# Value products of a cycle in two halves of 256 queries, with the output half in the first half's bank

## The chip, the cores and the metric

The kernel runs on one core of a Trainium2 chip. The metric is the device time of one execution in microseconds. The kernel before takes 947.69 us (median of three runs, 947.59 to 947.73). Its profile was taken in one execution of 946.93 us, of which the trace covers a span of 945.1 us; the mean granted TensorE clock was 0.997.

Engines are named as in the profile: PE is TensorE's matmul, PEld its weight load, DVE VectorE, ACT ScalarE, POOL GpSimd, SP SyncE.

## What is computed

The reference gates two branches over 2048 tokens of width 448. Branch A is attention with 16 query heads of 28 and a single key and value head, followed by an output projection; branch B is a token-shift mixer with two MLPs.

```python
q = (x @ wq).reshape(B, S, H, Dh)          # H = 16, Dh = 28
k = x @ wk; v = x @ wv                     # one head for all queries
p = softmax(einsum("bhqd,bkd->bhqk", q, k) * Dh ** -0.5)
a = einsum("bhqk,bkd->bhqd", p, v).reshape(B, S, H * Dh) @ wo
g = sigmoid((x * gate_w).sum(-1, keepdims=True))
return g * a + (1 - g) * b                 # b: the mixer, B_ref(x, ...)
```

## The kernel before

All arithmetic is in 32-bit floats; the score products run as three products of split operands (high by high, low by high, high by low). A first stage projects queries and the mixer's first half, a second one, up to about 400 us, runs the mixer's MLP. The change lies in the third stage, the attention, from there to the end.

**Units and cycles.** A unit u (0 to 15) is a block of 512 queries (u // 4) and a group of four heads (u % 4). Keys come in 16 tiles of 128. A cycle c handles two key tiles of a unit, so a unit has 8 cycles (i = 0 to 7) and the stage 128. The order of the work is written by hand; each engine runs its instructions in that order, and a tile framework adds the waits between engines.

**Banks.** PSUM has four single banks (`singles`) and two pairs of banks (`pairs`). Cycle c calls the singles s0, s1, s2, s3; in the next cycle the two halves of the list change places, so its s2 and s3 are this cycle's s0 and s1.

**One cycle, in PE's order.**

- A, the scores of the even key tile: heads 0 and 1 into s0 and s1, heads 2 and 3 into `pairs[0]`. Twelve matmuls (line 203), in three rounds of four; the four of a round use four row groups of the array.
- B, the same for the odd key tile, into s2, s3 and `pairs[1]`.
- V, the value products of the cycle before (line 861): for its two key tiles and four heads, `vext` (128 keys by 32 columns, one of which is ones and gives the softmax sum) against the probabilities of 512 queries, into the four column groups of s0. A 32-bit matmul of this kind is two instructions in the trace, so these are 16.
- W, a "job" (line 813): half of an output product, 224 of 448 columns of `wo` for 128 tokens, into s1. It is eight instructions. A unit's eight jobs are added to the list at i=4 of the next unit and are taken one in a cycle, two at i=5 (`TWICE`), none at i=2; the first unit has eight jobs of the mixer's last product (line 840) in their place, and the last one takes two a cycle from i=4.
- At i=2 (`MAX_AT`) there is in place of a job a product for the next unit's maxima (line 210), into s1.

**The other engines in a cycle.** ACT runs six exponentials (line 850): s0, s1, s2, s3, `pairs[1]`, each out of PSUM, and the two heads of `pairs[0]`, which DVE has copied to SBUF (line 889). DVE runs that copy, then the add of V's bank to the sum `o` of the unit (line 787, or a copy at the first time, line 785), then the job's add (line 832, or 844 for the mixer's). Between the copy and the add it has at i=1 a check and a reciprocal of the sums (lines 778 and 799), at i=3 the arrangement of the maxima (lines 236 to 240) and the normalisation (line 808), and at i=6 the split of the queries of a later unit (lines 194 and 195). At i=0 the SP queue sends the finished sums of the unit before out of `o` (`sums_begin`, line 792); after the add of the right half of an output tile's last group it sends the tile to the output (line 835).

Of the kernel before, what the change touches and what calls it, by code (L numbers as in the profile page):

```python
# [18 lines left out]
D = 448  # L19
# [5 lines left out]
NT = S // P  # L25
NF = F // P
NE = D // 32
NG = H // 4
# [13 lines left out]
def gated_mix_kernel(  # L42
# [12 lines left out]
    nc = tc.nc  # L55
# [688 lines left out]
    with tc.tile_pool(name="s3", bufs=1, reuse_waits="tile") as s3, \  # L744
# [8 lines left out]
        def bank(name):  # L753
            ps = banks.pop(0)
            banks.append(ps)
            return ps
# [20 lines left out]
            g = good[:, c:c + sums.shape[1]]  # L777
            nc.vector.scalar_tensor_tensor(g, sums, LIMIT, g, op0=ALU.is_le, op1=ALU.min)

        o_of = {}  # L780

        def values_end(u, pv):
            if u not in o_of:
                o_of[u] = s3.tile([P, 512], F32, tag="o", bufs=2, name=f"o_{u}")
                nc.vector.tensor_copy(o_of[u], pv)
            else:
                nc.vector.tensor_add(o_of[u], o_of[u], pv)  # L787

        def sums_begin(u):
            o = o_of.pop(u)  # L790
            rt = s3.tile([P, 16], F32, tag="rt", bufs=2, name=f"rt_{u}")
            nc.sync.dma_start(rt, o[0:128:32, :].rearrange("j (a b) -> j a b", b=16))
            return u, o, rt
# [16 lines left out]
        def by_columns(ps, a, t, w):  # L810
            for i in range(4):
                c = t * P + 32 * i
                nc.tensor.matmul(ps[32 * i:32 * i + 32, :], a[:, c:c + 32], w, start=True, stop=True,  # L813
                                 tile_position=(0, 32 * i))
# [3 lines left out]
        halves = [slice(0, D // 2), slice(D // 2, D)]  # L818

        def wo_products(u, t, ps, cols=whole):  # L820
            by_columns(ps[:, cols], on_of[u], t, wof[:, u % NG, cols])

        def wo_add(u, t, ps, cols=whole, end=None):
            b, g = divmod(u, NG)
            n = 4 * b + t
            before = x1[:, n, :] if g == 0 else ot_of[n]
            if g == 0 and cols.start == 0:
                ot_of[n] = s3.tile([P, D], F32, tag="ot", bufs=6, name=f"ot_{n}")
            if end:
                end(t, n, ps[:, cols], before)  # L830
                return
            nc.vector.scalar_tensor_tensor(ot_of[n][:, cols], ps[:, cols], gg[:, n:n + 1], before[:, cols],
                                           op0=ALU.mult, op1=ALU.add)
            if g == NG - 1 and cols.stop == D:
                nc.sync.dma_start(out[0, n * P:(n + 1) * P, :], ot_of[n])
# [1 line left out]
        weigh_x1(NT - 4, NT)  # L837

        def w4_products(t, ps, cols):
            by_columns(ps[:, cols], gf_late, t, w4_late[:, cols])  # L840

        def w4_add(t, ps, cols):
            n = NT - 4 + t
            nc.vector.scalar_tensor_tensor(x1[:, n, cols], ps[:, cols], gi[:, n:n + 1], x1[:, n, cols],
                                           op0=ALU.mult, op1=ALU.add)

        p_of = {}
# [6 lines left out]
            p_of[u * NT + kt] = p = s3.tile([P, 4, 512], F32, tag="p", bufs=PB, name=f"p_{u}_{kt}")  # L854
            return p

        def values(k, pv, first, last):
            u, kt = divmod(k, NT)
            p = p_of.pop(k)
            for j in range(4):  # L860
                nc.tensor.matmul(pv[32 * j:32 * j + 32, :], vext[:, kt, :], p[:, j],  # L861
                                 start=first, stop=last, tile_position=(0, 32 * j))

        jobs = [(w4_products, w4_add, (t,), cols) for t in range(4) for cols in halves]
        left, right, both = slice(0, 1), slice(1, 2), slice(2, 4)
# [2 lines left out]
        MAX_AT = 2  # L868
        TWICE = 5

        def run_jobs(ps, n):
            adds = []
            for _ in range(min(n, len(jobs))):
                products, add, args, cols = jobs.pop(0)
                products(*args, ps, cols)
                adds.append((add, args, cols))
            for add, args, cols in adds:
                add(*args, ps, cols)

        NC = NU * NT // 2  # L880
        for c in range(NC):
            u, i = divmod(c, NT // 2)
            k = 2 * c
            s0, s1, s2, s3_ = singles if c % 2 == 0 else singles[2:] + singles[:2]
            pa = score_tiles(u, 2 * i, s0, s1, pairs[0])
            exps(pa, left, s0.unsqueeze(1))
            exps(pa, right, s1.unsqueeze(1))
            if c < NC - 1:
                nc.vector.tensor_copy(pa[:, both], pairs[0])  # L889
            else:  # L890
                exps(pa, both, pairs[0])
            while later:
                later.pop(0)()
            if i == 1 and sums:
                norms.append(recip(*sums.pop()))
            if i == 1 and u == 0:
                q_begin(1)
                q_fetch(2)
            if i == 3 and norms:
                w = norms[0][0]  # L900
                norm(*norms.pop())
            if i == 6 and u + 2 < NU:
                q_begin(u + 2)
                q_fetch(u + 3)
            pb = score_tiles(u, 2 * i + 1, s2, s3_, pairs[1])
            exps(pb, left, s2.unsqueeze(1))
            exps(pb, right, s3_.unsqueeze(1))
            exps(pb, both, pairs[1])
            if c < NC - 1:
                exps(pa, both)  # L910
            if c:
                v = (c - 1) // (NT // 2)
                values(k - 2, s0, True, False)
                values(k - 1, s0, False, True)
                values_end(v, s0)
                if i == 0 and v < NU - 1:
                    sums.append(sums_begin(v))
            if i == 4 and u:
                jobs += [(wo_products, wo_add, (u - 1, t), cols) for t in range(4) for cols in halves]
            if i == MAX_AT and u + 1 < NU:  # L920
                max_part(u + 1, range(4), s1)
                later.append(lambda u=u: max_end(u + 1))
            elif c == 0:
                run_jobs(s0, 2)
                run_jobs(s1, 2)
            else:
                run_jobs(s1, 2 if i == TWICE or (u == NU - 1 and i > 3) else 1)
        pv = pairs[0][:, 0]
        values(2 * NC - 2, pv, True, False)
        values(2 * NC - 1, pv, False, True)  # L930
        assert not sums and not norms and not jobs and not later

        u = NU - 1
# [30 lines left out]
        def end(t, n, ps, before):  # L964
            if t == 1:
                nc.scalar.activation(y, ps, AF.Copy, scale=gg[:, n:n + 1])
                nc.gpsimd.tensor_tensor(ot_of[n], y, before, ALU.add)
            else:
                nc.vector.scalar_tensor_tensor(ot_of[n], ps, gg[:, n:n + 1], before, op0=ALU.mult, op1=ALU.add)
            queue = nc.scalar if t == 1 else nc.sync  # L970
            queue.dma_start(out[0, n * P:(n + 1) * P, :], ot_of[n])

        def tail_wo(t):
            wo_products(u, t, wo_banks[t])
            wo_add(u, t, wo_banks[t], end=end)

        def keep_warm(n):
            for _ in range(n):
# [39 lines left out]
        with tc.If(again > 0, label="redo"):  # L1018
            for b in range(NB):
                for g in range(NG):  # L1020
                    u = b * NG + g
                    q_fetch(u)
                    q_begin(u)
                    max_full(u, bank)
                    max_end(u)
                    pv = banks.pop(0)
                    for kt in range(NT):
                        ps = [bank(f"s2_{u}_{kt}_{j}") for j in range(4)]
                        scores(u, kt, ps)
                        p = s3.tile([P, 4, 512], F32, tag="p", bufs=PB, name=f"p2_{u}_{kt}")  # L1030
                        for j in range(4):
                            exps(p, slice(j, j + 1), ps[j].unsqueeze(1))
                        p_of[u * NT + kt] = p
                        values(u * NT + kt, pv, kt == 0, kt == NT - 1)
                    values_end(u, pv)
                    banks.append(pv)
                    norm(*recip(*sums_begin(u), False))
                    for t in range(4):
                        ps = bank(f"wo2_{u}_{t}")
                        wo_products(u, t, ps)  # L1040
                        wo_add(u, t, ps)

# [50 lines left out]
```

## Time and profile before

| | us |
|---|---|
| median of the runs (3) | 947.69 |
| profiled execution | 946.93 |
| its span | 945.1 |
| PE busy (modelled) | 936.3 |
| DVE busy | 504.1 |
| ACT busy | 637.3 |

A unit's eight cycles, u13 from 829.53 to 862.73 us, as busy time of the engines in each cycle (the columns are the stretch, its length, then busy time and instructions that began in it for PE, PEld, DVE, ACT and POOL, the granted clock, the share of the DMA engines and GB/s):

```
829.53:833.58 4.05, 4.05 (x52) 1.85 (x49) 2.28 (x4) 3.91 (x7) 0.00 (x0) 1.00 0.02 4
833.58:837.63 4.05, 4.05 (x52) 1.85 (x48) 2.60 (x6) 3.93 (x7) 0.00 (x0) 1.00 0.19 61
837.63:841.90 4.27, 4.27 (x48) 2.11 (x44) 2.50 (x4) 4.14 (x7) 0.00 (x0) 1.00 0.18 63
841.90:845.98 4.08, 4.08 (x49) 1.84 (x48) 3.33 (x8) 3.72 (x7) 0.00 (x0) 1.00 0.01 2
845.98:850.05 4.07, 4.07 (x52) 1.85 (x49) 2.29 (x4) 3.92 (x7) 0.00 (x0) 1.00 0.03 6
850.05:854.48 4.43, 4.43 (x62) 2.12 (x58) 2.66 (x4) 4.29 (x7) 0.00 (x0) 1.00 0.15 56
854.48:858.67 4.19, 4.19 (x53) 1.84 (x49) 3.35 (x7) 3.68 (x7) 0.00 (x0) 1.00 0.00 0
858.67:862.73 4.06, 4.06 (x53) 1.86 (x49) 2.29 (x4) 3.79 (x7) 0.00 (x0) 1.00 0.01 4
```

In an answer in order of time, a row has the start, the duration, the engine, the line, the operation with its tiles and form and, in brackets, how long the engine had stood idle before it and what ended that. Rows of one kind that lie close together are merged, with a count. A wait row has who waited for whom, the total in us, the number of times and the longest.

### The profile page before, as it was taken

What the parts mean: (1) busy time and instruction counts of PE and PEld (TensorE: products, weight loads), DVE (VectorE), ACT (ScalarE), POOL (GpSimd) and SP (SyncE); (2) the same over time, 40 slices, a digit from 0 to 9 for tenths busy, and PEclk for the clock granted to TensorE, in tenths of its full rate; (3) what the DMA queues carried; (4) which work ended last, traced back from release to release, by engine and by line L of the source; (5) the groups of instructions that cost most, each with busy time, mean ns of one, the idle gap of its engine ahead of it and who ended that gap; (6) DMA issues with size and microseconds to landing.
All of it is one profiled execution on the core that took longest, in us unless ns stands there. A gap on an engine that the chain in (4) does not pass through costs nothing.

```text
span 945.1 us, 19526 instructions
## 1 busy us (share of the span) xinstructions
PE 936.3 (99%) x8085; PEld 585.7 (62%) x8085; DVE 504.1 (53%) x829; ACT 637.3 (67%) x1006; POOL 80.8 (9%) x111
## 2 busy tenths in 40 slices
PE   9999999999999999999999999999999999999997
PEld 6788888888888888843444444444444444444442
DVE  4664464432432421266666666666656666666654
ACT  5532444322222222299999999999999999999993
POOL 3342500200000420110000000000000000000000
PEclk9999999999999999999999999999999999999998
DMA  9833452300300300010000000000010000010001
GB/s 313 283 83 76 138 167 85 93 10 1 84 1 1 84 1 1 12 50 24 12 23 14 23 32 33 24 13 23 15 51 23 14 23 12 31 40 16 6 13 43
DMA packets 40423, 47.05 MB, mean 50 GB/s; under 512 B 10120, under 2 KB 28488, under 8 KB 40328
## 3 DMA queue, kind: packets, MB, share of 16 engines
q1 hardware_dynamic: 37304, 40.27, 13.9%
q10 hardware_dynamic: 3024, 5.47, 1.6%
q8 instruction: 65, 1.06, 0.5%
q14 instruction: 30, 0.25, 0.1%
HBM read 32.56 MB, written 11.67 MB: 47 GB/s over the span
## 4 chain that ended last, share of the span: by engine, by line
PE 97%; ACT 1%; DMA 0%; DVE 0%; issue 0%; DVEq 0%
PE bank L861 24%; PE bank L203 22%; PE bank L813 5%; PE acc L682 5%; PE acc L684 5%; PE acc L683 5%; PE g L135 4%; PE g L136 4%; PE g L137 4%; PE pair L203 3%; PE hs L460 1%; PE hs L461 1%; PE g L138 1%; PE g L139 1%; ACT p L850 1%; PE h L135 1%
## 5 line engine op out<-in xcount | busy, mean ns | idle before, releaser
L850 ACT ACTIVATE p<-bank 128x512 f32<-128x512 f32 x512 | 265.1, 607 | 32.5 <-PE pair L203 17.3
L861 PE MATMUL bank<-p,vext 128*32 128x512 f32 x2032 | 244.3, 598 | 0.1
L889 DVE COPY p<-pair 128x1024 f32<-128x1024 f32 x127 | 155.5, 1225 | 22.7 <-PE pair L203 19.8
L672 ACT ACTIVATE gh<-g 128x512 fp32r<-128x512 f32 x55 | 32.9, 598 | 184.7 <-PE g L139 184.7
L787 DVE TENSOR_TENSOR o<-o,bank 128x512 f32<-128x512 f32 x111 | 76.3, 687 | 149.0 <-PE bank L861 135.1
L203 PE MATMUL bank<-qh,kh 32*128 32x512 f32 x512 | 146.3, 471 | 0.0
L850 ACT ACTIVATE p<-p 128x1024 f32<-128x1024 f32 x127 | 139.2, 1096 | 0.0
L850 ACT ACTIVATE p<-pair 128x1024 f32<-128x1024 f32 x129 | 136.8, 1060 | 0.0
L203 PE MATMUL bank<-ql,kh 32*128 32x512 f32 x512 | 130.6, 396 | 0.0
L861 PEld LDWEIGHTS bank<-p,vext 128*32 128x32 f32 x2032 | 53.0, 109 | 122.5 <-issue 76.0
L203 PE MATMUL pair<-qh,kh 32*128 32x512 f32 x512 | 128.0, 496 | 0.3 <-DVE x L738 0.3
L674 DVE TENSOR_TENSOR gl<-gf,gh 128x512 fp32r<-128x512 f32 x55 | 38.2, 695 | 166.5 <-ACT gf L673 166.5
L203 PE MATMUL bank<-qh,kl 32*128 32x512 f32 x512 | 126.9, 388 | 0.0
L203 PEld LDWEIGHTS bank<-qh,kh 32*128 32x128 f32 x512 | 69.0, 182 | 75.3 <-ACT p L850 40.9
L203 PE MATMUL pair<-qh,kl 32*128 32x512 f32 x512 | 101.0, 389 | 0.0
L203 PE MATMUL pair<-ql,kh 32*128 32x512 f32 x512 | 100.5, 387 | 0.0
L682 PE MATMUL acc<-w4h,gh 128*128 128x448 f32 x220 | 80.3, 365 | 0.0
L684 PE MATMUL acc<-w4h,gl 128*128 128x448 f32 x220 | 80.0, 364 | 0.0
L683 PE MATMUL acc<-w4l,gh 128*128 128x448 f32 x220 | 80.0, 363 | 0.0
L203 PEld LDWEIGHTS bank<-qh,kl 32*128 32x128 f32 x512 | 69.6, 183 | 8.4
L813 PEld LDWEIGHTS bank<-wof,on 128*32 128x32 f32 x992 | 32.0, 110 | 64.4 <-issue 32.1
L813 PE MATMUL bank<-wof,on 128*32 128x224 f32 (+1 forms) x992 | 67.5, 359 | 0.0
(199 smaller groups left out, 1470.3 us busy)
## 6 DMA issues: line engine op xcount, KB each, us to landing
qd<-qf ACTq DMA_DIRECT2D x16, 256.0 KB
rb<-rd SPq DMA_DIRECT2D x15, 256.0 KB
x<-in_x_dram SPq DMA_DIRECT2D x4, 896.0 KB
xd<-xt SPq DMA_DIRECT2D x16, 224.0 KB
w34raw<-in_w_dram SPq DMA_DIRECT2D x7, 512.0 KB
qr<-qd SPq DMA_DIRECT2D x64, 56.0 KB
out_dram<-ot SPq DMA_DIRECT2D x15, 224.0 KB
w34raw<-in_w_dram SPq DMA_DIRECT2D x7, 448.0 KB
```

Source lines behind the costliest of these rows:

```text
L135: nc.tensor.matmul(ps, wh[:, c, :], ah[:, c, :], start=(c == 0), stop=False)
L136: nc.tensor.matmul(ps, wh[:, c, :], al[:, c, :], start=False, stop=False)
L203: nc.tensor.matmul(ps[j], k[h, keys], q[h, :], start=(r == 0), stop=(r == 2), tile_position=(32 * j, 0))
L674: nc.vector.tensor_sub(gl, gf, f32(gh))
L682: nc.tensor.matmul(ps, gh[:, tok], w4h[i][:, k, :], start=(f == 0), stop=False)
L683: nc.tensor.matmul(ps, gh[:, tok], w4l[i][:, k, :], start=False, stop=False)
L684: nc.tensor.matmul(ps, gl[:, tok], w4h[i][:, k, :], start=False, stop=(f == stop))
L787: nc.vector.tensor_add(o_of[u], o_of[u], pv)
L813: nc.tensor.matmul(ps[32 * i:32 * i + 32, :], a[:, c:c + 32], w, start=True, stop=True, tile_position=(0, 32 * i))
L850: nc.scalar.activation(p[:, heads], p[:, heads] if source is None else source, AF.Exp, scale=SCALE)
L861: nc.tensor.matmul(pv[32 * j:32 * j + 32, :], vext[:, kt, :], p[:, j], start=first, stop=last, tile_position=(0, 32 * j))
L889: nc.vector.tensor_copy(pa[:, both], pairs[0])
```

## The change

In the cycles that have at most one job and no maxima, the value products run in two halves. Queries 0 to 255 of both key tiles go to the first 256 columns of s0, and DVE adds them to the first half of `o`. Queries 256 to 511 go to the first 256 columns of s1. The job's products come next, into columns 256 to 479 of s0, which the values no longer use; then DVE adds s1 to the second half of `o`, and then the job's result. Before, all values went to s0 and the job to s1, and DVE added them in that order. In these cycles V is 32 instructions of 256 columns in place of 16 of 512, and DVE has two adds of 256 columns in place of one of 512.

Cycles with two jobs (i=5, and from i=4 in the last unit) and those with the maxima (i=2) keep the one product of 512 queries. Where a unit begins (i=0), the DMA of the finished sums is now issued after the job's work, and not before it. The functions of the jobs take the part of the bank they write, in place of the bank and the columns; the path that repeats the attention with exact maxima, which runs only if a sum was out of range, is adapted to that.

```diff
-        o_of = {}
-        def values_end(u, pv):
+        o_of, fresh = {}, set()
+        def values_end(u, pv, qs=slice(0, 512)):
             if u not in o_of:
                 o_of[u] = s3.tile([P, 512], F32, tag="o", bufs=2, name=f"o_{u}")
-                nc.vector.tensor_copy(o_of[u], pv)
+                fresh.add(u)
+            o = o_of[u][:, qs]
+            if u in fresh:
+                nc.vector.tensor_copy(o, pv)
+                if qs.stop == 512:
+                    fresh.remove(u)
             else:
-                nc.vector.tensor_add(o_of[u], o_of[u], pv)
+                nc.vector.tensor_add(o, o, pv)
...
-        def values(k, pv, first, last):
-            u, kt = divmod(k, NT)
-            p = p_of.pop(k)
-            for j in range(4):
-                nc.tensor.matmul(pv[32 * j:32 * j + 32, :], vext[:, kt, :], p[:, j],
-                                 start=first, stop=last, tile_position=(0, 32 * j))
+        def values(ks, pv, qs=slice(0, 512)):
+            for k in ks:
+                u, kt = divmod(k, NT)
+                for j in range(4):
+                    nc.tensor.matmul(pv[32 * j:32 * j + 32, :], vext[:, kt, :], p_of[k][:, j, qs],
+                                     start=(k == ks[0]), stop=(k == ks[-1]), tile_position=(0, 32 * j))
+                if qs.stop == 512:
+                    p_of.pop(k)
...
-        def run_jobs(ps, n):
+        def job_products(ps, n):
             adds = []
             for _ in range(min(n, len(jobs))):
                 products, add, args, cols = jobs.pop(0)
-                products(*args, ps, cols)
-                adds.append((add, args, cols))
-            for add, args, cols in adds:
-                add(*args, ps, cols)
+                part = ps[:, 0:D // 2] if n == 1 else ps[:, cols]
+                products(*args, part, cols)
+                adds.append((add, args, part, cols))
+            return adds
...
-            if c:
-                v = (c - 1) // (NT // 2)
-                values(k - 2, s0, True, False)
-                values(k - 1, s0, False, True)
-                values_end(v, s0)
-                if i == 0 and v < NU - 1:
-                    sums.append(sums_begin(v))
...
-            if i == MAX_AT and u + 1 < NU:
-                max_part(u + 1, range(4), s1)
-                later.append(lambda u=u: max_end(u + 1))
-            elif c == 0:
+            if c == 0:
                 run_jobs(s0, 2)
                 run_jobs(s1, 2)
+                continue
+            v = (c - 1) // (NT // 2)
+            most = 2 if i == TWICE or (u == NU - 1 and i > 3) else 1
+            at_max = i == MAX_AT and u + 1 < NU
+            if at_max or (most == 2 and jobs):
+                values((k - 2, k - 1), s0)
+                values_end(v, s0)
+                if at_max:
+                    max_part(u + 1, range(4), s1)
+                    later.append(lambda u=u: max_end(u + 1))
+                else:
+                    run_jobs(s1, most)
             else:
-                run_jobs(s1, 2 if i == TWICE or (u == NU - 1 and i > 3) else 1)
+                q0, q1 = slice(0, 256), slice(256, 512)
+                values((k - 2, k - 1), s0[:, q0], q0)
+                values_end(v, s0[:, q0], q0)
+                values((k - 2, k - 1), s1[:, q0], q1)
+                adds = job_products(s0[:, q1], 1)
+                values_end(v, s1[:, q0], q1)
+                job_adds(adds)
+            if i == 0 and v < NU - 1:
+                sums.append(sums_begin(v))
```

`job_adds` runs the adds that `job_products` returned, and `run_jobs` is now the one after the other.

More of the change, by code (lines that the diff above doesn't have):

```diff
@@ L820, in wo_products @@
         def wo_products(u, t, ps, cols=whole):
-            by_columns(ps[:, cols], on_of[u], t, wof[:, u % NG, cols])
+            by_columns(ps, on_of[u], t, wof[:, u % NG, cols])
         def wo_add(u, t, ps, cols=whole, end=None):
@@ L829, in wo_add @@
             if end:
-                end(t, n, ps[:, cols], before)
+                end(t, n, ps, before)
                 return
-            nc.vector.scalar_tensor_tensor(ot_of[n][:, cols], ps[:, cols], gg[:, n:n + 1], before[:, cols],
+            nc.vector.scalar_tensor_tensor(ot_of[n][:, cols], ps, gg[:, n:n + 1], before[:, cols],
                                            op0=ALU.mult, op1=ALU.add)
@@ L839, in w4_products @@
         def w4_products(t, ps, cols):
-            by_columns(ps[:, cols], gf_late, t, w4_late[:, cols])
+            by_columns(ps, gf_late, t, w4_late[:, cols])
         def w4_add(t, ps, cols):
             n = NT - 4 + t
-            nc.vector.scalar_tensor_tensor(x1[:, n, cols], ps[:, cols], gi[:, n:n + 1], x1[:, n, cols],
+            nc.vector.scalar_tensor_tensor(x1[:, n, cols], ps, gi[:, n:n + 1], x1[:, n, cols],
                                            op0=ALU.mult, op1=ALU.add)
@@ L874, in run_jobs, with job_adds @@
                 products, add, args, cols = jobs.pop(0)
-                products(*args, ps, cols)
-                adds.append((add, args, cols))
-            for add, args, cols in adds:
-                add(*args, ps, cols)
+                part = ps[:, 0:D // 2] if n == 1 else ps[:, cols]
+                products(*args, part, cols)
+                adds.append((add, args, part, cols))
+            return adds
+        def job_adds(adds):
+            for add, args, part, cols in adds:
+                add(*args, part, cols)
+        def run_jobs(ps, n):
+            job_adds(job_products(ps, n))
         NC = NU * NT // 2
@@ L910, in gated_mix_kernel @@
                 exps(pa, both)
-            if c:
-                v = (c - 1) // (NT // 2)
-                values(k - 2, s0, True, False)
-                values(k - 1, s0, False, True)
-                values_end(v, s0)
-                if i == 0 and v < NU - 1:
-                    sums.append(sums_begin(v))
             if i == 4 and u:
                 jobs += [(wo_products, wo_add, (u - 1, t), cols) for t in range(4) for cols in halves]
-            if i == MAX_AT and u + 1 < NU:
-                max_part(u + 1, range(4), s1)
-                later.append(lambda u=u: max_end(u + 1))
-            elif c == 0:
+            if c == 0:
                 run_jobs(s0, 2)
                 run_jobs(s1, 2)
-            else:
-                run_jobs(s1, 2 if i == TWICE or (u == NU - 1 and i > 3) else 1)
+                continue
[10 more added lines that the diff above has]
+                    run_jobs(s1, most)
+            else:
+                q0, q1 = slice(0, 256), slice(256, 512)
[7 more added lines that the diff above has]
+                sums.append(sums_begin(v))
         pv = pairs[0][:, 0]
-        values(2 * NC - 2, pv, True, False)
-        values(2 * NC - 1, pv, False, True)
+        values((2 * NC - 2, 2 * NC - 1), pv)
         assert not sums and not norms and not jobs and not later
@@ L973, in tail_wo @@
         def tail_wo(t):
-            wo_products(u, t, wo_banks[t])
-            wo_add(u, t, wo_banks[t], end=end)
+            wo_products(u, t, wo_banks[t][:, whole])
+            wo_add(u, t, wo_banks[t][:, whole], end=end)
         def keep_warm(n):
@@ L1032, in gated_mix_kernel @@
                             exps(p, slice(j, j + 1), ps[j].unsqueeze(1))
-                        p_of[u * NT + kt] = p
-                        values(u * NT + kt, pv, kt == 0, kt == NT - 1)
+                        for j in range(4):
+                            nc.tensor.matmul(pv[32 * j:32 * j + 32, :], vext[:, kt, :], p[:, j],
+                                             start=(kt == 0), stop=(kt == NT - 1), tile_position=(0, 32 * j))
                     values_end(u, pv)
@@ L1038, in gated_mix_kernel @@
                     for t in range(4):
-                        ps = bank(f"wo2_{u}_{t}")
+                        ps = bank(f"wo2_{u}_{t}")[:, whole]
                         wo_products(u, t, ps)
```

## The prediction

> **What bounds the kernel now.** I read the page first: its engine line and the chain that ended last.
>
> ```profile
> span 945.1 us, 19526 instructions
> PE 936.3 (99%) x8085; PEld 585.7 (62%) x8085; DVE 504.1 (53%) x829; ACT 637.3 (67%) x1006; POOL 80.8 (9%) x111
> PE 97%; ACT 1%; DMA 0%; DVE 0%; issue 0%; DVEq 0%
> ```
>
> TensorE sets the end, but its busy time is modelled and hides short waits. So next I read the waits from 440 to 940 us, the attention stage that the change touches:
>
> ```profile
> PEld bank L861 <- ACT p L850: 42.9, 118, 0.5
> PEld bank L203 <- DVE ot L832: 19.6, 99, 0.3
> ```
>
> The second row is the wait to look at: a score product waits for the DVE add of an output half (L832). What it costs is seen only in the order of time. One whole cycle, u9 i=1, with the end of the one before it:
>
> ```profile
> 700.32 0.56 PE L813 MATMUL bank<-wof,on 128*32 128x224 f32 x8
> 700.63 0.69 DVE L787 TENSOR_TENSOR o<-o,bank 128x512 f32<-128x512 f32 x1 [1.57 <-PE bank L861]
> 700.82 0.50 PE L203 MATMUL bank<-qh,kh 32*128 32x512 f32 x2
> 701.24 0.45 DVE L832 SCALAR_TENSOR_TENSOR ot<-bank,gg,ot 128x224 f32<-128x224 f32 x1
> 701.35 0.59 SPq L792 DMA_DIRECT2D rt<-o  x1
> ...
> 701.62 0.61 PE L203 MATMUL bank<-qh,kh 32*128 32x512 f32 x2
> 701.74 0.18 PEld L203 LDWEIGHTS bank<-qh,kh 32*128 32x128 f32 x1 [0.16 <-DVE ot L832]
> ...
> 702.03 0.42 SPq L835 DMA_DIRECT2D out_dram<-ot  x1
> ...
> 702.63 0.16 PEld L861 LDWEIGHTS bank<-p,vext 128*32 128x32 f32 x8 [0.36 <-ACT p L850]
> 702.64 1.92 PE L861 MATMUL bank<-p,vext 128*32 128x512 f32 x16
> 703.09 0.13 PEld L861 LDWEIGHTS bank<-p,vext 128*32 128x32 f32 x4 [0.30 <-issue]
> 703.26 0.18 DVE L778 SCALAR_TENSOR_TENSOR good<-rt,good 128x16 f32<-128x16 f32 x1
> 703.52 0.13 PEld L861 LDWEIGHTS bank<-p,vext 128*32 128x32 f32 x4 [0.30 <-issue]
> ...
> 703.95 0.13 PEld L813 LDWEIGHTS bank<-wof,on 128*32 128x32 f32 x4 [0.30 <-ACT p L850]
> ...
> 704.38 0.56 PE L813 MATMUL bank<-wof,on 128*32 128x224 f32 x8
> 704.70 0.69 DVE L785 COPY o<-bank 128x512 f32<-128x512 f32 x1 [1.10 <-PE bank L861]
> 704.70 1.09 ACT L850 ACTIVATE p<-p 128x1024 f32<-128x1024 f32 x1
> 704.87 0.50 PE L203 MATMUL bank<-qh,kh 32*128 32x512 f32 x2
> ```
>
> The reader is to see this. A cycle is 704.87 - 700.82 = 4.05 us of PE work: scores of the even tile (A, from 700.82), scores of the odd tile (B, from 701.62, 0.80 after A), values (V, 702.63), the output half (W, 704.38). B's first product starts at 701.62, but the next ones stand until 701.74: bank s1 is held until the add of L832 ends at 701.24 + 0.45 = 701.69, 0.05 before. That add came late because it stood behind the 0.69 us add of the values, which could not start before all values were done (0.32 after W's start). Values run in batches of four at 0.43 us, the first 0.02 longer (702.64, 703.09, 703.52, 703.95, 704.38).
>
> **What takes the place of that wait.** V needs s0, and s0 is read by the first exponential of the cycle (window 701.86 to 702.0). A cycle that ACT sets shows how soon values follow such a read:
>
> ```profile
> 701.87 0.60 ACT L850 ACTIVATE p<-bank 128x512 f32<-128x512 f32 x1
> ```
> ```profile
> 432.51 0.68 ACT L850 ACTIVATE p<-bank 128x512 f32<-128x512 f32 x1
> ```
> ```profile
> 433.24 0.16 PEld L861 LDWEIGHTS bank<-p,vext 128*32 128x32 f32 x8 [0.47 <-ACT p L850]
> ```
>
> 432.51 + 0.68 = 433.19, and values load at 433.24: 0.05 later. So in u9 i=1 V could start at 701.87 + 0.60 + 0.05 = 702.52 and no sooner, however early the banks come free. Removing B's wait is worth 702.63 - 702.52 = 0.11 us in a cycle, not the 0.2 (19.6 / 99) that the waits view gives. PE itself would be ready a little before 702.52 (the groups of four that stood lose 0.12, and a fresh weight load), so this bound is the one that decides.
>
> **The change part by part.**
>
> *How many cycles.* By the loop, 127 cycles have values; 15 have the maximum (i=2), 19 have two jobs or the last of w4's: those 34 stay as before. 93 are split, 87 of them with an output half. Each split cycle frees the cycle after it. Of those cycles 86 waited on L832 and aren't bound by ACT: three in u0, two in u1, six in each of u2 to u14, three in u15. Gain: 86 x 0.11 = **-9.5 us**.
>
> *Values in halves.* Each split cycle issues 32 matmuls and 32 weight loads where it had 16 and 16. The nearest rows are the output halves, which have the same shape of weights and 224 columns:
>
> ```profile
> 853.61 0.94 PE L813 MATMUL bank<-wof,on 128*32 128x224 f32 x16
> 854.48 0.50 PE L203 MATMUL bank<-qh,kh 32*128 32x512 f32 x2
> ```
> ```profile
> 401.51 1.72 PE L813 MATMUL bank<-w_late,gf_late 128*32 128x224 f32 x32
> 403.16 0.51 PE L203 MATMUL bank<-qh,kh 32*128 32x512 f32 x2
> ```
>
> Sixteen take 854.48 - 853.61 = 0.87 until the next scores, eight took 704.87 - 704.38 = 0.49, so two more batches cost 0.38, 0.19 each. That is 0.43 x 224 / 512 = 0.188: loads hide under a batch of 224 columns. At 256 I take 0.216 a batch, 8 x 0.216 + 0.02 = 1.75 in place of 1.74 us. The upper bound is the first batch's surcharge of 0.02 in each of the eight (+0.16 a cycle, +14 us); the lower is no cost at all. I take 0.01: 87 x 0.01 = **+0.9 us**. Issue keeps up: 64 instructions ran in 403.16 - 401.51 = 1.65 us (26 ns each), and the new stretch has 80 in 2.13 (27 ns).
>
> The Trainium skill ("TensorEngine Tiling (Array Packing)", Instruction Overhead) charges about 60 cycles to each matmul; as an estimate by that page, 25 ns in four more batches is +0.1 us a split cycle and +9 us in all. The 0.19 us batches don't show it.
>
> *The add in halves.* The rows of the whole add, and of the same operation over 128 columns:
>
> ```profile
> L787 DVE TENSOR_TENSOR o<-o,bank x111: 686/687/689, 411.3 to 929.4; 128x512 f32<-128x512 f32 x111
> ```
> ```profile
> L982 DVE TENSOR_TENSOR oo<-o,pair x4: 278/279/289, 931.8 to 932.4; 128x128 f32<-128x128 f32 x4
> ```
>
> A line through both gives 279 + (687 - 279) / 3 = 415 ns for 256 columns: +0.14 of DVE time in a split cycle, on an engine that has over a microsecond idle there (1.57 before the add). What matters is when each ends. With V at 702.52: the second half starts 0.89 later (703.41), the first add 0.32 after that (703.73) and ends 704.15. W would start at V + 1.75 = 704.27. The second add starts at 704.59 and ends 705.01; W's last product ends 704.27 + 0.38 = 704.65, its add starts 0.3 later, is done by 705.39, and releases B at 705.44. B's turn is A + 0.80 = 704.27 + 0.49 + 0.80 = 705.56. So the old wait goes, with 0.12 to spare.
>
> *The new wait.* The output half now goes into the bank that the first add reads. No row shows whether PE's write to other columns of a bank is held for a read of it. Bounds: no hold, 0; hold, then W starts 0.05 (release) and 0.02 (load, as in V's first batch) after the add: 704.15 + 0.07 = 704.22, before 704.27. I take the hold, since all banks handed between PE and DVE here are waited for. It costs nothing in an ordinary cycle, **with only 0.05 us of cover**. Behind the held W stand the next cycle's scores and, through them, ACT. If the add took 0.45 (L832's row) and the four loads their 0.13 in full, W is at 703.73 + 0.45 + 0.05 + 0.13 = 704.36: 0.09 late.
>
> The Trainium skill ("PSUM — Partial Sum Buffer", PSUM bank collisions raise a hardware error) says that two engines must be kept apart in the same bank and quadrant even at other columns, which speaks for the hold; without it the sum would be that of the second rival below. No trace here shows such a pair.
>
> Where DVE has other work ahead of the first add, the cover is gone. Window 841.8 to 846 (i=3) and 854.4 to 858.7 (i=6):
>
> ```profile
> 843.75 0.16 PEld L861 LDWEIGHTS bank<-p,vext 128*32 128x32 f32 x8 [0.37 <-ACT p L850]
> ```
> ```profile
> 844.67 0.65 DVE L808 TENSOR_TENSOR on<-o,rb 128x512 f32<-128x512 f32 x1
> ```
> ```profile
> 856.43 0.16 PEld L861 LDWEIGHTS bank<-p,vext 128*32 128x32 f32 x8 [0.36 <-ACT p L850]
> ```
> ```profile
> 857.14 0.69 DVE L195 TENSOR_TENSOR ql<-qr,qh 128x512 fp32r<-128x512 f32 x1
> ```
>
> DVE starts the next instruction about 0.08 before the recorded end of the last (701.24 against 700.63 + 0.69). i=3: 844.67 + 0.65 - 0.08 + 0.42 + 0.07 = 845.73 against W's turn at 843.75 + 1.75 = 845.50: 0.23 late, 13 times (u2 to u14), **+3.0 us**. i=6: 857.14 + 0.69 - 0.08 + 0.42 + 0.07 = 858.24 against 858.18: 0.06, 13 times, **+0.8 us**.
>
> *The sums' DMA moved behind the job* (i=0). o is whole earlier than before (705.01 - 702.52 = 2.49 after V against 2.7), so SP's rt leaves earlier, except in u4, u8 and u12, where the job's out DMA is now ahead of it: it waits for the output add (V + 2.87) and takes 0.42, so rt leaves at V + 3.3, about 0.5 late. The check of L778 follows rt by 703.26 - 701.35 = 1.91; it and the reciprocal then stand in front of the first add, which ends some 0.27 too late for W: 3 x 0.27 = **+0.8 us**.
>
> The repeat path's edits aren't executed, and the last cycle's values keep their order: nothing.
>
> Sum: -9.5 + 0.9 + 3.0 + 0.8 + 0.8 = **-4.0 us**, I take -3.7 for rounding in the 0.11 and u15. Against the profiled execution, 946.93 us (its span 945.1), that is 943.2; against the median 947.69, which is 0.76 above it, **944.0 us**.
>
> **The rivals.**
>
> *The hold isn't there* (W may run beside the read). For: different columns. The delays of i=3, i=6 and the DMA vanish, 4.6 us: 947.69 - 8.3 = 939.4. Chance 0.13.
>
> *The hold binds in every split cycle* (the other side). One place, W behind the first add; it decides once W is over 3.7 / 87 = 0.043 us later than I have it, which is as much as my cover of 0.05 running out by 0.04. At the upper 0.09 it costs 87 x 0.09 = 7.8: 947.69 - 3.7 + 7.8 = 951.8. For: the cover is thin. Against: each piece is from a row, and the upper ones are for other operations. Chance 0.20.
>
> *Short batches cost more.* Eight surcharges of 0.02: 944.0 + 14 - 0.9 = 957. It decides from 0.005 a batch. Against: the 0.19 us batches. Chance 0.08.
>
> *ACT takes over.* Its six instructions need 3.76 us back to back:
>
> ```profile
> 432.51 2.15 ACT L850 ACTIVATE p<-bank 128x512 f32<-128x512 f32 x4
> ...
> 435.33 1.20 ACT L850 ACTIVATE p<-p 128x1024 f32<-128x1024 f32 x1
> 436.27 2.20 ACT L850 ACTIVATE p<-bank 128x512 f32<-128x512 f32 x4
> ```
>
> The new cycle is 3.95, so there is 0.19 left. If the first exponential then took 0.68 as at 432.51, the gain is 0.03 in place of 0.11: 944.0 + 6.9 = 950.9; half of it, 947.5. Chance 0.09.
>
> **How the numbers follow.** Forecast 0.50, with its own range 942 to 946.5; the rivals 0.13, 0.20, 0.08, 0.09. The range 939 to 952 leaves out the short batches, the top of the hold and a little below 939.4. About 0.2% (1.9 us) is what a measurement of this kernel can tell from no change: faster takes 0.46 of the forecast and the 0.13; same takes 0.04 of it, 0.06 of the hold, 0.05 of ACT; slower the rest, 0.26.
>
> **What would show it.** Right: values that start 0.05 after the first exponential's end in the cycles after a split one; no PE wait on L832 there; values in 1.75 us; W with no gap after them in ordinary cycles, and gaps of some 0.2 only at i=3. Wrong: a PE wait on the add of o ahead of W in every split cycle, values over 1.8 us, or W running while that add reads its bank.

## The result and the profile after

The changed kernel takes 944.74 us (median of eight runs, 942.98 to 945.81) against 947.64 us of the kernel before (median of eight, 947.34 to 949.92); the ratio, estimated from all these runs, is 0.9966, with a 95% interval of 0.9956 to 0.9977. The forecast was 944.0. Its profiled execution took 944.86 us, with a span of 943.1.

The page of the changed kernel, first its head and then the chain that ended last by engine:

```profile
span 943.1 us, 22620 instructions
PE 928.3 (98%) x9573; PEld 618.1 (66%) x9573; DVE 516.7 (55%) x922; ACT 636.9 (68%) x1006; POOL 81.1 (9%) x111
PE 94%; ACT 3%; issue 1%; DMA 0%; DVE 0%; ACTq 0%; DVEq 0%
```

PE still sets the end, but the chain now passes through ACT for 3% of the span (1% before), as it would if a wait for ACT took the old one's place. The waits from 440 to 940 us (value adds are now lines 788 and 792, output halves 818 with their add in 837, values 866, exponentials 855):

```profile
PEld bank L866 <- ACT p L855: 53.7, 119, 0.7
PEld bank L818 <- DVE o L792: 20.3, 70, 0.5
PEld bank L203 <- DVE ot L837: 5.3, 17, 0.3
PEld bank L818 <- DVE o L788: 4.0, 14, 0.5
```

The wait of a score product on the output add has gone from 99 times to 17, which are in the cycles after two jobs. In its place stands a wait of the output half on the value add, 84 times. How little of that is lost is seen only in order of time. Two cycles, u9 i=0 and i=1:

```profile
696.77 0.50 PE L203 MATMUL bank<-qh,kh 32*128 32x512 f32 x2
...
697.57 0.40 PE L203 MATMUL bank<-qh,kh 32*128 32x512 f32 x2
697.58 0.39 PE L203 MATMUL pair<-qh,kh 32*128 32x512 f32 x2
...
698.48 1.93 PE L866 MATMUL bank<-p,vext 128*32 128x256 f32 x32
699.67 0.42 DVE L792 TENSOR_TENSOR o<-o,bank 128x256 f32<-128x256 f32 x1 [0.60 <-PE bank L866]
700.15 0.21 PEld L818 LDWEIGHTS bank<-wof,on 128*32 128x32 f32 x8 [0.22 <-DVE o L792]
700.23 0.56 PE L818 MATMUL bank<-wof,on 128*32 128x224 f32 x8
700.53 0.42 DVE L792 TENSOR_TENSOR o<-o,bank 128x256 f32<-128x256 f32 x1 [0.44 <-PE bank L866]
700.72 0.50 PE L203 MATMUL bank<-qh,kh 32*128 32x512 f32 x2
...
700.87 0.45 DVE L837 SCALAR_TENSOR_TENSOR ot<-bank,gg,ot 128x224 f32<-128x224 f32 x1
...
701.35 0.36 SPq L840 DMA_DIRECT2D out_dram<-ot  x1
...
701.76 0.59 SPq L797 DMA_DIRECT2D rt<-o  x1
...
702.43 1.93 PE L866 MATMUL bank<-p,vext 128*32 128x256 f32 x32
703.66 0.18 DVE L778 SCALAR_TENSOR_TENSOR good<-rt,good 128x16 f32<-128x16 f32 x1 [0.64 <-DMA rt<-o]
703.75 0.25 DVE L804 RECIPROCAL rr<-rt 128x16 f32<-128x16 f32 x1
703.91 0.36 DVE L788 COPY o<-bank 128x256 f32<-128x256 f32 x1
...
704.33 0.16 PEld L818 LDWEIGHTS bank<-wof,on 128*32 128x32 f32 x8 [0.45 <-DVE o L788]
704.33 0.58 PE L818 MATMUL bank<-wof,on 128*32 128x224 f32 x8
```
```profile
697.83 0.60 ACT L855 ACTIVATE p<-bank 128x512 f32<-128x512 f32 x1
```

In i=0 all four first products of B start together (697.57, 697.58). Values start at 698.48, 0.05 after the first exponential's end at 697.83 + 0.60. They take 700.23 - 698.48 = 1.75 us. The output half's loads wait for the first add, which ends at 700.09, and go at 700.15; its matmuls start at 700.23, exactly when the values are through. So the 0.22 of that wait costs nothing. The cycle is 700.72 - 696.77 = 3.95 us in place of 4.05.

ACT itself has not become the limit. Its rows around the start of i=1:

```profile
699.75 1.06 ACT L855 ACTIVATE p<-pair 128x1024 f32<-128x1024 f32 x1
700.65 1.09 ACT L855 ACTIVATE p<-p 128x1024 f32<-128x1024 f32 x1
701.77 2.06 ACT L855 ACTIVATE p<-bank 128x512 f32<-128x512 f32 x4
```

The first exponential begins 701.77 - 700.72 = 1.05 after A, as it did before the change (701.87 - 700.82). Where ACT does not wait, it starts an instruction 0.16 before the recorded end of the last (700.65 against 699.75 + 1.06); here it starts 0.03 after it (700.65 + 1.09 = 701.74). By these rows, as an estimate, it has some 0.19 in hand.

In i=1 the same order costs 0.15: the sums' DMA left at 701.76, behind the output's; the check came at 703.66, the first copy at 703.91, and the output half started at 704.33 and not at 702.43 + 1.75 = 704.18.

The median lengths by place in the unit, u2 to u13, each from the first score product of a cycle to that of the next:

| i | cycle before | cycle after | V after A, before | after | W after V, before | after |
|---|---|---|---|---|---|---|
| 0 | 4.05 | 3.95 | 1.816 | 1.709 | 1.741 | 1.751 |
| 1 | 4.05 | 3.95 | 1.819 | 1.705 | 1.741 | 1.751 |
| 2 (maxima) | 4.27 | 4.15 | 1.825 | 1.707 | 1.854 | 1.854 |
| 3 | 4.07 | 4.31 | 1.842 | 1.843 | 1.741 | 1.953 |
| 4 | 4.06 | 3.95 | 1.828 | 1.707 | 1.741 | 1.751 |
| 5 (two jobs) | 4.43 | 4.32 | 1.814 | 1.705 | 1.741 | 1.741 |
| 6 | 4.20 | 4.26 | 1.966 | 1.969 | 1.741 | 1.776 |
| 7 | 4.06 | 3.95 | 1.827 | 1.708 | 1.741 | 1.751 |

Six cycles get shorter, i=3 and i=6 longer. These two follow a cycle that is not split, so their values do not come earlier. At i=3 (u8, DVE and PEld) the reason for the loss stands in four rows:

```profile
678.75 0.65 DVE L813 TENSOR_TENSOR on<-o,rb 128x512 f32<-128x512 f32 x1
679.32 0.41 DVE L792 TENSOR_TENSOR o<-o,bank 128x256 f32<-128x256 f32 x1
```
```profile
677.84 1.45 PEld L866 LDWEIGHTS bank<-p,vext 128*32 128x32 f32 x32 [0.36 <-ACT p L855]
679.79 0.16 PEld L818 LDWEIGHTS bank<-wof,on 128*32 128x32 f32 x8 [0.49 <-DVE o L792]
```

The add begins 1.48 after the values where it begins 1.19 after them in u9 i=0, because the normalisation is in front of it.

**Two things ahead of the steady cycles.** The span is 2.0 us shorter, but the attention itself is shorter by more. Its first score product, before and after, and the first projections of the program:

```profile
399.14 0.50 PE L203 MATMUL bank<-qh,kh 32*128 32x512 f32 x2
```
```profile
401.69 0.50 PE L203 MATMUL bank<-qh,kh 32*128 32x512 f32 x2
```
```profile
4.92 3.74 PE L313 MATMUL q<-xkv,wqraw 128*128 128x512 f32 x8 [0.28 <-DMA wqraw<-in_wq_dram]
```
```profile
5.34 5.85 PE L313 MATMUL q<-xkv,wqraw 128*128 128x512 f32 x8 [0.70 <-DMA wqraw<-in_wq_dram]
```

From there to the end (with the spans to three places, 945.124 and 943.055) it is 545.98 us before and 541.36 after: 4.62 less. The 2.55 of later begin come from eight matmuls at the start, code that the change does not touch: 5.85 us for 3.74, and 0.42 of later data.

And in u0 i=1 the changed kernel loses a microsecond (5.29 us, before 4.29):

```profile
408.95 0.43 DVE L194 CAST qh<-qr 128x512 fp32r<-128x512 f32 x1 [0.94 <-DMA qr<-qd]
...
410.01 0.75 DVE L788 COPY o<-bank 128x256 f32<-128x256 f32 x2
```
```profile
410.49 0.16 PEld L818 LDWEIGHTS bank<-w_late,gf_late 128*32 128x32 f32 x8 [1.27 <-DVE o L788]
```

DVE waits for a DMA of queries there, with the value copies queued behind it and, now, the job's products behind them. This is not in every execution: the profile of `max_late` has it too (5.48), that of `warm_after` does not (4.30).

### The profile page after: what moved, and what is told of

It reads as the page before. It is cut to its first block, busy times and chain, and to the rows that moved or that the text cites. A ratio compares the mean times of both kernels' runs of the same rounds, so it can differ in the third digit from the quotient of the medians.

```text
span 943.1 us, 22620 instructions
## 1 busy us (share of the span) xinstructions
PE 928.3 (98%) x9573; PEld 618.1 (66%) x9573; DVE 516.7 (55%) x922; ACT 636.9 (68%) x1006; POOL 81.1 (9%) x111
## 4 chain that ended last, share of the span: by engine, by line
PE 94%; ACT 3%; issue 1%; DMA 0%; DVE 0%; ACTq 0%; DVEq 0%
PE bank L866 25%; PE bank L203 19%; PE bank L818 6%; PE acc L682 5%; PE acc L684 5%; PE acc L683 5%; PE g L135 4%; PE g L136 4%; PE g L137 4%; ACT p L855 3%; PE pair L203 2%; PE hs L460 1%; PE hs L461 1%; PE g L138 1%; PE g L139 1%; PE h L135 1%
## 5 line engine op out<-in xcount | busy, mean ns | idle before, releaser
L866 PE MATMUL bank<-p,vext 128*32 128x256 f32 (+1 forms) x3520 | 245.3, 415 | 4.7 <-ACT p L855 1.3
L866 PEld LDWEIGHTS bank<-p,vext 128*32 128x32 f32 x3520 | 101.4, 109 | 125.7 <-ACT p L855 57.5
L792 DVE TENSOR_TENSOR o<-o,bank 128x256 f32<-128x256 f32 (+1 forms) x188 | 88.1, 469 | 110.2 <-PE bank L866 99.6
L203 PE MATMUL bank<-qh,kh 32*128 32x512 f32 x512 | 125.5, 450 | 0.0
L203 PE MATMUL pair<-qh,kh 32*128 32x512 f32 x512 | 118.1, 457 | 0.3 <-DVE x L738 0.3
L203 PE MATMUL bank<-ql,kh 32*128 32x512 f32 x512 | 111.0, 394 | 0.0
L203 PE MATMUL bank<-qh,kl 32*128 32x512 f32 x512 | 108.7, 389 | 0.0
L203 PEld LDWEIGHTS bank<-qh,kh 32*128 32x128 f32 x512 | 54.0, 182 | 62.3 <-issue 22.3
L818 PE MATMUL bank<-wof,on 128*32 128x224 f32 (+1 forms) x992 | 68.2, 362 | 0.2
L135 PE MATMUL g<-ah,w3h 128*128 128x512 f32 x168 | 65.8, 392 | 0.0
L136 PE MATMUL g<-al,w3h 128*128 128x512 f32 x168 | 65.7, 391 | 0.0
```

The costliest lines, as they stand in the source:

```text
L135: nc.tensor.matmul(ps, wh[:, c, :], ah[:, c, :], start=(c == 0), stop=False)
L136: nc.tensor.matmul(ps, wh[:, c, :], al[:, c, :], start=False, stop=False)
L203: nc.tensor.matmul(ps[j], k[h, keys], q[h, :], start=(r == 0), stop=(r == 2), tile_position=(32 * j, 0))
L792: nc.vector.tensor_add(o, o, pv)
```

## Experiments

**What the short matmuls cost: `shapes`.** The kernel before with V in halves in the cycles that the change splits, both halves into s0, and one add as before.

```diff
-                values(k - 2, s0, True, False)
-                values(k - 1, s0, False, True)
+                if i == MAX_AT or i == TWICE or (u == NU - 1 and i > 3):
+                    values(k - 2, s0, True, False)
+                    values(k - 1, s0, False, True)
+                else:
+                    for qs in (slice(0, 256), slice(256, 512)):
+                        for kk in (k - 2, k - 1):
+                            vkt = kk % NT
+                            for j in range(4):
+                                nc.tensor.matmul(s0[32 * j:32 * j + 32, qs], vext[:, vkt, :], p_of[kk][:, j, qs],
+                                                 start=(kk == k - 2), stop=(kk == k - 1), tile_position=(0, 32 * j))
+                    p_of.pop(k - 2)
+                    p_of.pop(k - 1)
```

> The kernel before, with the value products of the same cycles issued as 32 instructions of 256 columns, both halves into the same bank, and one add over all 512 as before; nothing else moves. It prices the short matmuls by themselves. Theory: loads hide under a batch of 256 columns, values take 1.75 us in place of 1.74, 93 cycles, so +1 us on the kernel before, about 948.6. Rival (short batches pay a surcharge of 0.01 to 0.02 us each): values 1.83 to 1.90 us, +8 to +15 us, 956 to 963.

Measured: 948.96 us (median of 11 runs), ratio 1.0021 (1.0012 to 1.0030) to the kernel before. The ratio is above that of the medians, since the runs lie in two groups: six at 948.4 to 949.0, five at 949.8 to 950.9. One cycle's values and output half in order of time:

```profile
699.75 1.93 PE L921 MATMUL bank<-p,vext 128*32 128x256 f32 x32
701.50 0.56 PE L813 MATMUL bank<-wof,on 128*32 128x224 f32 x8
```

701.50 - 699.75 = 1.75 us. Doubling the instructions costs 0.01 us a cycle, and the rival of dear short batches falls: it asked for 1.83 at least, and for 956 us.

**Why i=3 got longer: `max_late`.** The changed kernel with DVE's arrangement of the maxima at i=4.

```diff
-            while later:
+            while later and i == 4:
```

> The changed kernel with one thing moved: DVE's three instructions that arrange the maxima (0.55 us) run at i=4 and not at i=3. Theory: at i=3 the output half is late because DVE has 0.55 + 0.65 us of other work ahead of the first add of the values, and W is held for that add. Without the 0.55 the normalisation ends before the first half is ready, so values to output half at i=3 falls from 1.95 to 1.75 us and the cycle from 4.31 to about 4.08, in 13 units: 3 us less than the changed kernel, about 941.7. Rival: i=3 is long because of the wait on the maxima's reduction ahead of B, which this does not touch: 1.95 and 944.7 stay.

Measured: 941.43 us (939.96 to 942.42, 5 runs), ratio 0.9936 (0.9923 to 0.9950) to the kernel before. u8 i=3, in order of time:

```profile
674.58 1.93 PE L866 MATMUL bank<-p,vext 128*32 128x256 f32 x32
...
674.95 0.68 DVE L813 TENSOR_TENSOR on<-o,rb 128x512 f32<-128x512 f32 x1
...
675.77 0.42 DVE L792 TENSOR_TENSOR o<-o,bank 128x256 f32<-128x256 f32 x1
676.24 0.22 PEld L818 LDWEIGHTS bank<-wof,on 128*32 128x32 f32 x8 [0.21 <-DVE o L792]
676.33 0.56 PE L818 MATMUL bank<-wof,on 128*32 128x224 f32 x8
```

The add begins 1.19 after the values again, the output half 1.75, and the median cycle at i=3 is 4.09. The profiles give 13 x (4.310 - 4.087) = 2.9 us for it, so what i=3 lost was DVE's queue ahead of the add. The medians differ by 3.3; part of that is the start of the program, which came early in the profiled execution of `max_late` (see below). i=4, with the moved 0.55 us, stays at 3.95.

**What sets the start of the values: `half_exp`.** The changed kernel with half of one exponential left out.

```diff
-            exps(pa, left, s0.unsqueeze(1))
+            nc.gpsimd.memset(pa[:, 0, 256:512], 0.0)
+            nc.scalar.activation(pa[:, 0, 0:256], s0[:, 0:256], AF.Exp, scale=SCALE)
```

> The changed kernel with the first exponential of each cycle (head 0 of the even tile, out of s0) over 256 of its 512 queries; GpSimd writes zeros for the rest, so half of that head's weights are left out. Theory: in the cycles after a split one the values start 0.05 us after that exponential lets go of s0 (1.65 after the first score product, values at 1.705). With 256 columns it takes about 0.24 less, and then PE's own order decides: its last score product starts at 1.28 and values follow 0.32 after such a product, so 1.60. That is 0.10 a cycle in 84 cycles, 8 to 9 us less than the changed kernel, about 936. Rival: it is PE's change from rows to columns that sets the start, and the exponential only happens to end then: values stay at 1.705 and the time at 944 to 945.

Measured: 936.22 us (4 runs), ratio 0.9874 (0.9857 to 0.9891), 8.5 us less than the changed kernel. Its u9 i=0, with the exponential of 256 columns from a narrow window of ACT:

```profile
691.78 0.50 PE L203 MATMUL bank<-qh,kh 32*128 32x512 f32 x2
...
693.38 1.93 PE L866 MATMUL bank<-p,vext 128*32 128x256 f32 x32
```
```profile
692.86 0.39 ACT L901 ACTIVATE p<-bank 128x256 f32<-128x256 f32 x1
```

Values start 693.38 - 691.78 = 1.60 after A. The exponential ends at 693.25, more than 0.05 before, so here PE's own order is the bound. In the changed kernel it is ACT's read of s0, as the prediction had it.

**Whether a bank is held as a whole: `job_s1`.** The changed kernel with the output half in the other bank.

```diff
-                adds = job_products(s0[:, q1], 1)
+                adds = job_products(s1[:, q1], 1)
```

> The changed kernel with the output half in the free columns of s1, the second half's bank, and not of s0. Theory (a bank is handed over as a whole between PE and DVE, whatever the columns): W no longer waits for the first add, so the 0.2 us at i=3 go; but the second add, behind W in the program, now has to wait until W is done, 0.38 later, and the output add behind it frees the bank at about 3.27 after V's start against a turn of B at 3.04. B waits again, values start at about 1.93 in place of 1.705, six times a unit: some 15 us more than the changed kernel, 955 to 961, slower than before. Rival (only overlapping columns are held): the second add runs beside W, no wait on either, and i=3, i=6 and the first unit get shorter: about 940.

Measured: 959.98 us (958.0 to 960.84, 4 runs), ratio 1.0121 (1.0102 to 1.0141). u9 i=0:

```profile
704.96 0.50 PE L203 MATMUL bank<-qh,kh 32*128 32x512 f32 x2
...
705.16 0.42 DVE L792 TENSOR_TENSOR o<-o,bank 128x256 f32<-128x256 f32 x1 [0.82 <-PE bank L818]
705.50 0.45 DVE L837 SCALAR_TENSOR_TENSOR ot<-bank,gg,ot 128x224 f32<-128x224 f32 x1
...
705.99 0.18 PEld L203 LDWEIGHTS bank<-qh,kh 32*128 32x128 f32 x1 [0.28 <-DVE ot L837]
...
706.89 1.93 PE L866 MATMUL bank<-p,vext 128*32 128x256 f32 x32
...
708.64 0.56 PE L818 MATMUL bank<-wof,on 128*32 128x224 f32 x8
```

The second add, which reads only values, waits for the output half in other columns of its bank (0.82 <-PE bank L818). Behind it the output add is late, B stands until 705.99, and values start 1.93 after A, in place of 1.71. So the hold is real and goes by banks: it is a wait that the program sets between the engines, and no run here shows what would happen without it. Which bank the job goes to decides the sign of the whole change: 15 us lie between s0 and s1.

**The start of the program: `warm_after` and `warm_before`.** Both kernels with 20 warming matmuls.

```diff
-    for _ in range(16):
+    for _ in range(20):
         nc.tensor.matmul(wps[:, 0:256], warm[:, 0:P], warm, start=True, stop=True)
```

> The changed kernel with 20 instead of 16 warming matmuls at its start. In the profile of the changed kernel the attention takes 4.6 us less than before, but it begins 2.5 us later, since the first eight projection products (L313) run at 0.85 us each, five of them, where the kernel before has 0.43. Theory: that is the start-up of TensorE's clock, which depends on how long PE stood idle before its first data came, and not the change. With the warming up to 5.3 us those products run at 0.43 us, the attention begins at 399.5 to 400, and the median falls to about 943.2 with a spread of under 1.5 us. Rival: the longer program itself costs the time ahead of the attention: its begin stays at 401.7 and the median at 944.7.

> The kernel before with 20 instead of 16 warming matmuls. Theory (start-up of the clock): most of its executions already find a warm clock, so 947.5 to 948.0, with no outliers at 949.9; the ratio of the changed to the kernel before, both with 20, is 0.9952 (4.5 us). Rival (the program's length): the ratio stays 0.9966.

Measured: the changed kernel 942.63 us (942.04 to 943.49, 5 runs), the kernel before 947.63 (946.94 to 948.43, 11 runs); 942.63 / 947.63 = 0.9947. The ratios to the kernel before as it was are 0.9951 (0.9937 to 0.9964) and 1.0001 (0.9992 to 1.0010). The first projections of `warm_after`, and, for comparison, those of `max_late`, which has the 16:

```profile
5.28 3.70 PE L313 MATMUL q<-xkv,wqraw 128*128 128x512 f32 x8 [0.39 <-DMA wqraw<-in_wq_dram]
```
```profile
5.39 3.70 PE L313 MATMUL q<-xkv,wqraw 128*128 128x512 f32 x8 [1.12 <-DMA wqraw<-in_wq_dram]
```

With 20, the eight products take 3.70 us, the attention begins at 400.09, and the change is worth 5.0 us by the medians.

That it is the clock, the traces show by their own clock records, which carry times; the views print only a mean, and count time without a record as full clock. The first record, at full clock, begins at 9.70 us in the changed kernel and at 5.03 in the kernel before; with 20 warming matmuls it begins at 4.14 and 4.68. In each of these traces the matmuls go over to twice the pace about then.

One part of the theory falls: it is not the length of the idle time. `max_late` stood 1.12 us and ran at full pace, the changed kernel 0.70 and did not; in `max_late` the record begins at 3.75, while the warming matmuls still run. Of the six profiled executions with 16, three begin late: that of the changed kernel, `half_exp` (9.52) and `job_s1` (9.38). The three with 20 all begin early, and so does `shapes` (4.05) with 16. The Trainium skill ("TensorE: Matmul & The Clock Gate", Part 1) says that the clock is released and withdrawn by activity in windows of 3.4 us that run freely. That would fit early and late starts after the same warming, but no run here shows the windows.

Nor is it shown why the changed kernel, with 16, spreads over 2.8 us where most of the runs before lie within 0.7. `shapes`, which starts as the kernel before does, spreads over some 2.5.

**All of it together: `best`.** 20 warming matmuls; maxima at i=4; the query split at i=5; the second cycle whole; the sums' DMA ahead of the output add. The first two edits are those of `warm_after` and `max_late`; the others:

```diff
-            if i == 6 and u + 2 < NU:
+            if i == 5 and u + 2 < NU:
...
-            if at_max or (most == 2 and jobs):
+            if at_max or c == 1 or (most == 2 and jobs):
...
                 values_end(v, s1[:, q0], q1)
+                if i == 0 and v < NU - 1:
+                    sums.append(sums_begin(v))
                 job_adds(adds)
-            if i == 0 and v < NU - 1:
-                sums.append(sums_begin(v))
```

> The changed kernel with everything that the traces named: 20 warming matmuls; the maxima's arrangement at i=4; the query split at i=5, a cycle that isn't split; the second cycle of the stage whole, since its DVE waits for a DMA of queries ahead of the values; the sums' DMA issued ahead of the output add. Theory: 942.6 (the changed kernel with 20 warming matmuls) less 3.0 at i=3, 0.7 at i=6, 0.5 in u5, u9 and u13: about 938.4, and a ratio to the kernel before of 0.990. Rival (the moved DVE work comes back at its new place, ahead of the values' add at i=5 or of the maxima's rows): no less than 939.5 to 941.

Measured: 938.40 us (938.01 to 939.58, 4 runs), ratio 0.9902 (0.9886 to 0.9919). i=3 has a median of 4.09 and i=6 of 4.21 us, u9 i=1 is 3.95. It beats both kernels, the changed one with 20 warming matmuls by 4.2 us.

## Why the prediction was right, term by term

| Term | predicted, us | measured in the profiles, us |
|---|---|---|
| 86 cycles without B's wait | -9.5 (0.11 each) | -9.9 (0.115, the mean of the six cycles of the table) |
| 87 cycles of short matmuls | +0.9 | +0.9 (1.751 for 1.741) |
| i=3, 13 times | +3.0 | +2.9 (4.310 - 4.074 - 0.01 each) |
| i=6, 13 times | +0.8 | +0.7 (4.260 - 4.199 - 0.01 each) |
| sums' DMA, 3 times | +0.8 | +0.6 (0.16 to 0.22) |
| u0 i=1 | none | +1.0 |
| sum | -4.0 | -3.8 |

The stage measured 4.62 less. Most of the rest, 0.66 of 0.8, is in three cycles of the kernel before (u3 i=5, u6 i=1, u8 i=5), which are longer than their like by 0.14, 0.15 and 0.37 us. They are no accident of one execution: the profiles of `shapes` and `warm_before` have the same three cycles at the same lengths (4.57, 4.20 and 4.79 us, within 0.01), and the changed kernel has none of them. The prediction had no term for this. In u8 i=5 of the kernel before it was a value add that came 0.37 late. Why, the trace does not say, nor whether the change removes such delays or moves them: single long cycles stand elsewhere in `job_s1` (u7 i=5, 4.89) and `best` (u10 i=3, 4.38).

- **The bound behind the removed wait** was the step that mattered most: 0.11 us a cycle and not the 0.2 of the waits view, since the values next wait for ACT to let go of s0. `half_exp` shows it: 0.10 more came free as soon as that read got shorter.
- **The price of halving** was a scaled row of the output halves, 0.19 us to 0.216 a batch, and `shapes` measured just that.
- **The hold by banks** was assumed, and `job_s1` shows it. The rival in which it binds in every cycle did not come: the first add began 1.19 after the values (predicted 1.21), and loads went 0.08 before the matmuls' turn.
- **ACT did not take over:** the 0.19 us that the prediction left it are still there, by the rows above.
- **Three slips.** The working says that without the hold the sum would be that of the second rival; it is the first one that has no hold. The DMA's term falls in u5, u9 and u13, not in u4, u8 and u12: at i=0 the jobs are still those of two units back. And the prediction went through DVE's extra work at i=1, 3 and 6 of the steady units but not of the first one, where the query split waits for a DMA: 1.0 us in this execution, nothing in that of `warm_after`.
- **The time itself** came out 0.7 above the forecast, and that it came so near is in part luck. In this execution the late start of the program took back 2.55 us and u0 i=1 another 1.0; the three long cycles gave 0.66. None of these stood in the sum. With 20 warming matmuls in both kernels the change is 5.0 us by the medians; in the two profiled executions, where u0 i=1 costs nothing, the time from the first score product to the end falls by 5.7 (546.38 to 540.65).

## What to carry to other kernels

When a wait is removed, look for the second to last condition of the same instruction and price the gain by the distance to it, not by the wait's own total. An add that releases a bank for the next product is on the critical path as soon as something else stands ahead of it in its engine's queue: list that engine's extra work cycle by cycle, the first cycles too. Two uses of one PSUM bank in different columns were still one hand-over between the engines here, so put the second use into the bank whose reader finishes first.

## What was not expected of the hardware

The first projections of the changed kernel ran 0.85 us apart, half of the pace of 0.43 that they have before, though the granted clock reads 1.00 for the first 12 us of both executions:

```profile
0.00:12.00 12.00, 10.26 (x29) 5.47 (x30) 4.69 (x8) 6.14 (x10) 4.25 (x15) 1.00 0.83 284
```
```profile
0.00:12.00 12.00, 10.68 (x40) 6.78 (x41) 4.50 (x8) 6.24 (x11) 4.25 (x15) 1.00 0.84 296
```

These are the busy times by stretch of the kernel after and of the one before; the third column from the end is the granted clock, and the counts of matmuls, 29 and 40, give the pace away. The column misleads because the first clock record of these traces, at full clock, begins only at 9.70 us after and at 5.03 before, and time without a record counts as full. The products show the same turn: those of the kernel after start 0.85 apart up to 8.91 us and 0.43 apart from 9.74. So at the start of a program read the clock from the pace of the matmuls; a 1.00 in that column does not show it.
